# Linear attention with a gated feed-forward: tails of two batches computed together, loads held behind a transposition, and a reordered head

## The chip, the cores and the metric

The kernel runs on one core of one Trainium2 chip. The metric is the device time of one execution in microseconds (us), and a smaller number is better. Executions of this kernel agree within some 0.3%. The profile also records the clock that TensorE was granted, as a share of full speed.

## The reference, cut to what matters

Linear attention over 8 batches of 8 heads, with 576 rows of 64 columns each, feeds a layer with 2048 hidden units. Between the two matrix products of that layer stands a swish with one beta for each hidden unit. All inputs and the output are fp32.

```python
def phi(x):                              # elu(x) + 1
    return np.where(x > 0, x, np.exp(x) - 1.0) + 1.0
q_p, k_p = phi(q), phi(k)                # q, k, v: (8, 8, 576, 64)
kv  = np.einsum('bhsd,bhse->bhde', k_p, v)
z   = np.sum(k_p, axis=2)
num = np.einsum('bhsd,bhde->bhse', q_p, kv)
den = np.einsum('bhsd,bhd->bhs', q_p, z)[..., None] + 1e-06
x   = (num / den).transpose(0, 2, 1, 3).reshape(4608, 512)
h   = x @ w_in                           # (512, 2048)
g   = h * (1.0 / (1.0 + np.exp(-beta * h)))
out = g @ w_out                          # (2048, 512)
```

## The kernel before

A batch has 576 rows: four blocks of 128 and a tail of 64. The feed-forward runs in nine phases of 512 rows: one for the four blocks of each batch, and a last one for the eight tails together. While TensorE works on the feed-forward of batch b, the attention of batch b+1 is slipped in between its matmuls, by lists ("plans") that name a point in the stream and what to do there. The whole schedule is made by hand. The names that matter: `kv_bd` is kv with its denominators, `q_pT` the transposed phi(q), `xs` a normalised block of attention output and `xT` its transposition, `vaug` is v with a column of ones.

The numerators and their norm, with one matmul group for each block, the tail included:

```python
def num_mm(b, t):
    n = rows(t)                                   # 128, or 64 for the tail (t == 4)
    nps = att_banks()
    for p in range(KC):                           # KC = 4
        c0 = (p % 2) * 2 * (D + 1)
        nc.tensor.matmul(
            nps[:n, p // 2, c0 : c0 + 2 * (D + 1)],
            st[b, "qT"][:, t, p, :n],
            kv_bd[b % 2][p // 2][:, p % 2], ...)

def num_norm(b, t):
    n = rows(t)
    ...                                           # den + 1e-6, reciprocal, multiply -> xs
    if by_dma(b):                                 # batches 3 to 7
        nc.sync.dma_start_transpose(out=x_dst(b, t), in_=...xs...[:n])
```

The head loads batch 0 through GpSimd's queue, which in this kernel casts fp32 to bf16 on the way:

```python
    load_nine(k9, k)
    load_nine(q9, q, j1=4)
    ...
    load_nine(v9, v, j1=6)
    load_nine(v9, v, j0=6)
    load_nine(q9, q, j0=4)
    for i in range(4):
        nc.gpsimd.dma_start(out=w_in_sb[i], in_=w_in_v[:, :, i * 512 : (i + 1) * 512])
    load_w_out(0)
    ...
```

The plans of batches 1 and 2 (cut):

```python
    w_out_scale(2)
    phi(1, 1)                       # phi of k
    v_copy(1)
    phi(1, 0)                       # phi of q
    y_phase_wide(0, {
        4: [F(load_next, 3)],
        9: [F(kv_mm, 1), F(kv_evac, 1), F(w_out_scale, 3)],
        10: [F(q_trans, 1, 0, 1, wide=True), F(q_trans, 1, 2, 3, wide=True)],
        ...
    })
    h_phase(1, ..., {
        0: [F(x_trans, 1, 2), F(num_mm, 1, 4), F(num_norm, 1, 4)],
        1: [F(x_trans, 1, 3)],
        3: [F(x_trans, 1, 4)],
        ...
        12: [F(v_copy, 2), F(load_next, 4)],      # batch 4's k, q, v
    })
    ...
    y_phase_wide(1, {
        1: [F(phi, 2, 0), F(q_trans_dma, 2), F(phi, 2, 1)],
        6: [F(kv_mm, 2), F(kv_evac, 2)],
        11: [F(num_mm, 2, 0), F(num_norm, 2, 0)],
        12: [F(num_mm, 2, 1), F(num_norm, 2, 1), F(x_trans, 2, 0, wide=True)],
        ...
    })
```

Of the kernel before, what the change touches and what calls it, by code (L numbers as in the profile page):

```python
# [16 lines left out]
def kernel(  # L17
# [18 lines left out]
    NJ = 4  # L36
# [80 lines left out]
    def nine(a, spec):  # L117

        names = " ".join(spec)
        flat = a.rearrange("p a b c -> p (a b c)")  # L120
        size = {"h": HH, "j": N9, "d": D}
        n = size["h"] * size["j"] * size["d"]
        return flat[:, 0:n].rearrange(f"p ({names}) -> p {names}", **size)

    q9 = nine(xqk[0][:, 0], "hjd")
    k9 = nine(xqk[0][:, 1], "hjd")
    v9 = nine(vraw[0], "hjd")

    def load_nine(dst, src, h0=0, h1=HH, j0=0, j1=N9):
        for g in range(2):  # L130
            nc.gpsimd.dma_start(  # L131
                out=dst[g * TAIL : (g + 1) * TAIL, h0:h1, j0:j1, :].rearrange(
                    "p h j d -> p h (j d)"
                ),
                in_=src[0, g * HH + h0 : g * HH + h1, :, :]
                .rearrange("h (p j) d -> p h j d", j=N9)[:, :, j0:j1, :]
                .rearrange("p h j d -> p h (j d)"),
            )
# [4 lines left out]
    nc.vector.memset(g_sb[0][:, FC - 1, :], 0.0)  # L143
    clear_tail(1)
    nc.vector.memset(vraw[1][TAIL:P, :, NJ, :], 0.0)
    beta_row = consts.tile([FC, P], F32)
    nc.sync.dma_start(out=beta_row, in_=moe_beta.rearrange("(c p) -> c p", p=P))
# [3 lines left out]
    load_nine(k9, k)  # L151
    load_nine(q9, q, j1=4)
    make_identity(nc, identity)
    make_identity(nc, ident16)
    load_nine(v9, v, j1=6)
    load_nine(v9, v, j0=6)
    load_nine(q9, q, j0=4)
    for i in range(4):
# [9 lines left out]
    kv_bd = [  # L168
        [consts.tile([P, 2, 2, D + 1], BF16, name=f"kv_bd{i}{g}") for g in range(2)]
        for i in range(2)  # L170
    ]
    for i in range(2):
        for g in range(2):
            nc.vector.memset(kv_bd[i][g], 0.0)
# [32 lines left out]
    def w_out_scale(i, dve=True):  # L207
        for c in range(4):
            ff = 4 * i + c
            dst, src, by = w_out_sb[i][:, c, :], w_out_f[i][c // 2][:, c % 2, :], rbeta[:, ff : ff + 1]  # L210
            if dve:
# [36 lines left out]
    x0 = {0: q9, 1: k9}  # L248
# [4 lines left out]
    def exp0(a, j0, j1):  # L253
        if j0 == 0:
            st["e0", a] = work9("e", bufs=3)
        nc.scalar.activation(  # L256
            st["e0", a][:, j0:j1].rearrange("p j h d -> p h j d"), x0[a][:, :, j0:j1],
            ACTF.Exp,
        )

    def relu0(a, j0, j1):
        if j0 == 0:
            st["r0", a] = work9("r")
        nc.vector.tensor_scalar(
            st["r0", a][:, j0:j1].rearrange("p j h d -> p h j d"), x0[a][:, :, j0:j1],
# [3 lines left out]
    def phi0(a, j0, j1):  # L269
        nc.vector.tensor_tensor(  # L270
            st["p0"][a][:, j0:j1], st["r0", a][:, j0:j1], st["e0", a][:, j0:j1], ALU.min
        )

    def q_trans0(t, banks, c0):


        for jj in range(2 if t < NJ else 1):
            for a in range(2):
                for g in range(2):
# [4 lines left out]
                        st["p0"][0][gs, 2 * t + jj, 2 * a : 2 * a + 2, :],  # L284
# [4 lines left out]
    def q_out0(t, banks, c0, dve):  # L289
        n = rows(t)  # L290
        src = banks[:, :, c0 : c0 + 2 * P].rearrange("p g (a n) -> p g a n", a=2)
        dst = st[0, "qT"][:, t].rearrange("p (g a) n -> p g a n", g=2)
        copy(dst[:, :, :, :n], src[:, :, :, :n], dve)
# [5 lines left out]
    def kv_mm0(kvp, j0, j1, of_v):  # L299


        for j in range(j0, j1):
            for a in range(2):
                for g in range(2):
# [4 lines left out]
                        st["p0"][1][gs, j, 2 * a : 2 * a + 2, :],  # L309
# [6 lines left out]
    def kv_evac0(kvp):  # L316
        for g in range(2):
            for i in range(2):
                gs = slice(i * D, (i + 1) * D)
                copy(  # L320
                    kv_bd[0][g][gs, :, i, :],
# [29 lines left out]
    def kv_evac(b):  # L351
        for i in range(2):
            for g in range(2):
                gs = slice(g * D, (g + 1) * D)
                nc.vector.tensor_copy(  # L355
                    kv_bd[b % 2][i][gs, :, g, :], st[b, "kvp"][gs, 2 * i : 2 * i + 2, :]
                )
# [16 lines left out]
    def q_trans(b, *ts, wide=False, dve=False):  # L374

        n, m = rows(ts[0]), len(ts)
        tp = tr_bank(wide).rearrange("p (t c n) -> p t c n", t=2, c=KC)
# [7 lines left out]
        copy(st[b, "qT"][:, ts[0] : ts[0] + m, :, :n], tp[:, 0:m, :, :n], dve)  # L385
# [7 lines left out]
    def num_mm(b, t):  # L393
        n = rows(t)
        nps = att_banks()
        st[b, "n", t] = nps
        for p in range(KC):
            c0 = (p % 2) * 2 * (D + 1)
            nc.tensor.matmul(  # L399
                nps[:n, p // 2, c0 : c0 + 2 * (D + 1)],  # L400
                st[b, "qT"][:, t, p, :n],
                kv_bd[b % 2][p // 2][:, p % 2],
                start=True, stop=True, skip_group_check=True,
            )

    def num_norm(b, t):
        n = rows(t)
# [10 lines left out]
        if by_dma(b):  # L418
# [4 lines left out]
    def x_dst(b, t):  # L423
        if t < NJ:
            return xT[b % 3][:, t]
        return xT_tail[:, :, b * TAIL : (b + 1) * TAIL]

    def x_trans(b, t, wide=False, dve=False):
        n = rows(t)
# [51 lines left out]
    out0 = out[0:S, :].rearrange("(p j) m -> p j m", j=N9)  # L481

    def tail_rows(b):
        if b == 0:
            return out0[:, N9 - 1, :]
        return out[b * S + MAIN : (b + 1) * S, :]

    def store(b, t, y_sb):
        if b < B:
            if b == 0:  # L490
                for i in range(2):
                    nc.sync.dma_start(
                        out=out0[:, 2 * t + i, :], in_=y_sb[i * TAIL : (i + 1) * TAIL, :]
# [77 lines left out]


# [10 lines left out]
    def F(f, *a, **k):  # L583
        return lambda: f(*a, **k)

    begin(0)
    st["warm"] = mm_bank([P, 512])
    warm(10)
    beta_trans()
    make_beta()  # L590
    warm(20)
    st["p0"] = [
        nine(st[0, "p"][:, a].rearrange("p j (h d) -> p j h d", h=H), "jhd")
        for a in range(2)
    ]
    exp0(1, 0, 5)
    exp0(1, 5, N9)
    exp0(0, 0, 4)
    relu0(1, 0, 5)
    relu0(1, 5, N9)  # L600
    phi0(1, 0, 5)
    relu0(0, 0, 4)
    phi0(1, 5, N9)
    phi0(0, 0, 4)
    kvp = [mm_bank([P, 512]) for _ in range(2)]
    kv_mm0(kvp, 0, N9, False)
    qb = att_banks(BF16)
    q_trans0(0, qb, 0)
    q_trans0(1, qb, 256)
    q_out0(0, qb, 0, False)  # L610
    q_out0(1, qb, 256, False)
# [164 lines left out]
```

## Time and profile before

| | before |
|---|---|
| time, median of 3 runs | 296.43 us (296.33 to 296.48) |
| profiled execution | 296.85 us, of which 295.1 us is the span that the profile shows |
| TensorE busy | 283.9 us, 96% of the span |
| floor of the 1152 feed-forward units | 249 us |

The prediction below shows the lines that tell what bounds this kernel. Two more views follow. The first is the queue of the Sync engine (start in us, length in us, engine, operation) between 40 and 90 us, and the second is GpSimd over 52 to 66 us, where it issues batch 4's loads.

```profile
70.30 5.46 SPq L388 DMA_TRANSPOSE q_pT<-qk_p  x1
```

```profile
53.50 0.88 POOL L72 DMA_DIRECT2D xqk<-in_k_dram  x1 [1.58 <-ACT y_sb L513]
...
63.29 0.88 POOL L72 DMA_DIRECT2D vraw<-in_v_dram  x1 [2.28 <-DMA xqk<-in_q_dram]
```

The transposition of batch 2's q is issued at 70.30 us and is on the queue for 5.46 us. By the view of its tile it has landed 9.0 us after its issue, at 79.3, which is exactly when TensorE's first numerators of batch 2 start. Batch 4's loads are issued from 53.50 us on and are still moving then.

### The profile page before, as it was taken

Reading aid. Unit: us, or ns where it says so; the run is one execution under the profiler, and the core shown is the slowest. Engines: PE = TensorE matmul, PEld = TensorE weight load, DVE = VectorE, ACT = ScalarE, POOL = GpSimd, SP = SyncE. Lnnn points to the kernel's source line nnn. Section 1 sums busy time; section 2 is a strip of 40 time slices with the busy share of each in tenths; the row PEclk is TensorE's granted clock in tenths of the full one; section 3 lists DMA queues with packets and bytes.
Section 4 is the critical chain, followed back from the end, with each engine's and each line's share of the span. In section 5 each row is a group of like instructions: output and inputs, shape, how many; then the busy total and the mean of one; then the engine's idle time right before and its main releaser. Section 6 shows DMA issues by size and latency. Waiting matters only on the chain.

```text
span 295.1 us, 4750 instructions
## 1 busy us (share of the span) xinstructions
PE 283.9 (96%) x1891; PEld 143.9 (49%) x1912; DVE 124.0 (42%) x261; ACT 175.1 (59%) x234; POOL 52.7 (18%) x72
## 2 busy tenths in 40 slices
PE   8879999999999999999999999999999999999994
PEld 3557445644465544445444544454445444444444
DVE  4765488504365174616461646154715400110012
ACT  2788786889988780778087907790770077018500
POOL 8924474540003200330023000000000000000000
PEclk9999999999999999999999999999999999999999
DMA  7999999999637993699369945024502400120032
GB/s 103 196 207 343 256 272 192 256 193 192 89 142 100 175 131 113 130 174 154 98 129 159 159 109 124 2 71 116 127 0 72 118 36 0 38 90 16 0 73 71
DMA packets 72310, 37.09 MB, mean 126 GB/s; under 512 B 40912, under 2 KB 66784, under 8 KB 72288
## 3 DMA queue, kind: packets, MB, share of 16 engines
q0 software_dynamic: 38912, 20.45, 47.9%
q1 hardware_dynamic: 33216, 16.20, 22.9%
q8 instruction: 15, 0.25, 0.3%
q10 hardware_dynamic: 160, 0.13, 0.2%
q14 instruction: 7, 0.06, 0.1%
HBM read 36.71 MB, written 9.44 MB: 156 GB/s over the span
## 4 chain that ended last, share of the span: by engine, by line
PE 76%; DMA 9%; POOL 4%; ACT 4%; issue 4%; DVE 1%; ACTq 0%; POOLq 0%; DVEq 0%
PE mm L453 37%; PE mm L505 33%; DMA xT<-in_moe_w_out_dram 5%; DMA vraw<-in_v_dram 4%; PE att L399 3%; ACT e L229 2%; POOL xqk L131 1%; PE att L344 1%; PE mm L537 1%; POOL w_in L159 1%; ACT L229 1%; POOL vraw L131 1%; ACT g L445 1%; DVE qk_p L242 0%; POOL xqk L111 0%
## 5 line engine op out<-in xcount | busy, mean ns | idle before, releaser
L445 ACT ACTIVATE g<-mm,beta_c 128x512 bf16<-128x512 f32 (+2 forms) x156 | 97.3, 633 | 88.4 <-PE mm L453 88.1
L505 PE MATMUL mm<-w_out,g 128*128 128x512 bf16 x541 | 126.7, 379 | 1.2 <-issue 0.3
L453 PE MATMUL mm<-xT,w_in 128*128 128x512 bf16 (+2 forms) x560 | 108.1, 349 | 1.4 <-DMA w_in<-in_moe_w_in_dram 1.1
L453 PEld LDWEIGHTS <-w_in 128*128 128x128 bf16 x656 | 61.9, 98 | 62.4 <-DMA w_in<-in_moe_w_in_dram 1.2
L505 PEld LDWEIGHTS <-g 128*128 128x128 bf16 x560 | 53.0, 98 | 58.2
L515 DVE COPY y_sb<-mm 128x512 f32<-128x512 f32 x27 | 18.7, 691 | 70.6 <-PE mm L505 69.1
L229 ACT ACTIVATE e<-xqk 128x2560 bf16<-128x2560 bf16 x14 | 31.9, 2329 | 0.1
L415 DVE TENSOR_TENSOR xs<-att,rden 128x512 bf16<-128x512 f32 (+1 forms) x40 | 27.6, 689 | 1.4
L242 DVE TENSOR_TENSOR qk_p<-r,e 128x2560 bf16<-128x2560 bf16 x14 | 20.9, 1490 | 13.1 <-ACT e L229 12.4
L355 DVE CAST kv_bd<-att 64x130 bf16<-64x130 f32 x28 | 8.2, 292 | 32.2 <-PE att L344 31.8
L72 POOL DMA_DIRECT2D vraw<-in_v_dram x7 | 6.4, 909 | 84.2 <-DVE vaug L370 78.5
L413 DVE TENSOR_SCALAR den<-att 128x8 f32<-128x8 f32 (+1 forms) x40 | 6.5, 161 | 32.0 <-PE att L399 31.9
L399 PE MATMUL att<-kv_bd,q_pT 128*128 128x130 bf16 (+1 forms) x160 | 15.8, 221 | 1.1 <-DVE kv_bd L370 0.7
L399 PEld LDWEIGHTS <-q_pT 128*128 128x128 bf16 (+1 forms) x160 | 11.6, 100 | 10.7 <-DVE xs L415 2.4
L453 PE MATMUL mm<-xT_tail,w_in 128*128 128x512 bf16 x63 | 13.9, 379 | 0.1
L237 DVE TENSOR_SCALAR r<-xqk 128x2560 bf16<-128x2560 bf16 x14 | 11.6, 834 | 3.8 <-DMA xqk<-in_q_dram 2.3
L575 PE MATMUL mm<-g 128*128 128x512 bf16 x34 | 9.9, 452 | 1.2 <-DVE g L143 1.2
L229 ACT ACT_TABLE_LOAD x7 | 9.0, 1283 | 0.1
L414 DVE RECIPROCAL rden<-den 128x8 f32<-128x8 f32 (+1 forms) x40 | 8.1, 202 | 1.4
L72 POOL DMA_DIRECT2D xqk<-in_k_dram x7 | 6.9, 984 | 6.3 <-DMA w_in<-in_moe_w_in_dram 2.8
L76 POOL DMA_DIRECT2D xqk<-in_k_dram x7 | 7.4, 1057 | 1.5 <-DMA w_in<-in_moe_w_in_dram 1.3
L256 ACT ACTIVATE e<-xqk 128x1280 bf16<-128x1280 bf16 (+1 forms) x4 | 4.4, 1155 | 5.4 <-DMA xqk<-in_k_dram 5.3
(71 smaller groups left out, 140.0 us busy)
## 6 DMA issues: line engine op xcount, KB each, us to landing
out_dram<-y_sb SPq DMA_DIRECT2D x28, 256.0 KB, 2.3
xqk<-in_k_dram POOLq DMA_DIRECT2D x7, 512.0 KB, 10.7
xqk<-in_q_dram POOLq DMA_DIRECT2D x7, 512.0 KB, 11.3
vraw<-in_v_dram POOLq DMA_DIRECT2D x7, 512.0 KB, 11.3
w_in<-in_moe_w_in_dram POOLq DMA_DIRECT2D x4, 512.0 KB, 11.0
g<-in_moe_w_out_dram POOLq DMA_DIRECT2D x4, 512.0 KB, 10.9
out_dram<-y_sb SPq DMA_DIRECT2D x14, 128.0 KB, 5.2
xqk<-in_moe_w_out_dram POOLq DMA_DIRECT2D x2, 512.0 KB, 14.4
```

What stands on the lines that cost most here:

```text
L72: eng.dma_start(out=dst[:, :, 0:NJ, :].rearrange("p h j d -> p h (j d)"), in_=src[b, :, 0:MAIN, :].rearrange("h (p j) d -> p h (j d)", j=NJ),)
L229: nc.scalar.activation(st[b, "e", a][:, h0:h1], xqk[b % NX][:, a, h0:h1], ACTF.Exp)
L237: nc.vector.tensor_scalar(st[b, "r", a][:, h0:h1], xqk[b % NX][:, a, h0:h1], 0.0, 1.0, ALU.max, ALU.add)
L242: nc.vector.tensor_tensor(st[b, "p"][:, a].rearrange("p j (h d) -> p h j d", h=H)[:, h0:h1], st[b, "r", a][:, h0:h1], st[b, "e", a][:, h0: ...
L355: nc.vector.tensor_copy(kv_bd[b % 2][i][gs, :, g, :], st[b, "kvp"][gs, 2 * i : 2 * i + 2, :])
L399: nc.tensor.matmul(nps[:n, p // 2, c0 : c0 + 2 * (D + 1)], st[b, "qT"][:, t, p, :n], kv_bd[b % 2][p // 2][:, p % 2], start=True, stop=True ...
L415: nc.vector.tensor_mul(xs[:n], nv[:, :, :, 0:D], rden[:n, :, :, None].to_broadcast([n, 2, 4, D]))
L445: nc.scalar.activation(g_sb[b % 2][:, ff, c0:c1], hp[:, c0:c1], ACTF.Silu, scale=beta_c[:, ff : ff + 1],)
L453: nc.tensor.matmul(hp[:, c0:c1], w_in_sb[ff // 4][:, kc, (ff % 4) * P : (ff % 4 + 1) * P], x[:, t0:t1, kc, :] if b < B else x[:, kc, c0:c1 ...
L505: nc.tensor.matmul(yp, g_sb[b % 2][:, ff, t * P : (t + 1) * P], w_out_sb[ff // 4][:, ff % 4, :], start=(ff == 0), stop=(ff == FC - 1),)
L515: nc.vector.tensor_copy(y_sb, yp)
L575: nc.tensor.matmul(st["warm"], g_sb[0][:, FC - 1, 0:P], g_sb[0][:, FC - 1, :], start=True, stop=True, skip_group_check=True,)
```

## The change

The intent was to take the last few us out of an already full TensorE. The tails of two neighbouring batches are computed as one block of 2 x 64 rows (joint tails), so half of the tail work vanishes. Batch 4's loads are held until batch 2's q has been transposed, by a one-element copy on GpSimd that reads the transposed q. In the head, k arrives through two queues, and kv and q are taken in smaller pieces. In batch 1, q is transposed ahead of kv. In batch 2, copies of x^T move from ScalarE to VectorE. (Beta's small load moves from Sync's queue to ScalarE's.) The diff, cut to its core:

```diff
 # the head
+    load_nine(k_last, k, KF, N9, eng=nc.sync)          # 4 of 9 parts of k, fp32, Sync's queue
-    load_nine(k9, k)
-    load_nine(q9, q, j1=4)
+    load_nine(x9[1][:, :, 0:KF], k, 0, KF)             # KF = 5
+    load_nine(x9[0][:, :, 0:QF], q, 0, QF)             # QF = 4
...
-    warm(20)
+    warm(15)
...
 # kv copied out in two pieces (was four)
 def kv_evac(b):
-    for i in range(2):
-        for g in range(2): ...
+    for g in range(2):
+        gs = slice(g * D, (g + 1) * D)
+        nc.vector.tensor_copy(kv_bd[b % 2][gs, :, g, :], st[b, "kvp"][gs])
...
 # joint tails
 def num_mm(b, t):
     for p in range(KC):
         c0 = (p % 2) * 2 * (D + 1)
+        for i in range(1 if t < NJ else 2):
+            bb, n, r0 = (b, P, 0) if t < NJ else (b - 1 + i, TAIL, i * TAIL)
             nc.tensor.matmul(
-                nps[:n, p // 2, c0 : c0 + 2 * (D + 1)],
-                st[b, "qT"][:, t, p, :n],
-                kv_bd[b % 2][p // 2][:, p % 2],
+                nps[r0 : r0 + n, p // 2, c0 : c0 + 2 * (D + 1)],
+                st[bb, "qT"][:, t, p, :n],
+                kv_bd[bb % 2][:, p],
...
-        if by_dma(b):
+        if by_dma(b) or t == NJ:
...
 # held loads
+    def hold(a):
+        nc.gpsimd.tensor_copy(held, a)
+    def held_load(b, n):
+        hold(st[n, "qT"][0:1, NJ, KC - 1, 0:1])
+        load_next(b)
...
 # batch 1
-    v_copy(1)
     phi(1, 0)
+    v_copy(1, 0, HH)
+    v_copy(1, HH, H, dve=False)
-        9: [F(kv_mm, 1), F(kv_evac, 1), F(w_out_scale, 3)],
-        10: [F(q_trans, 1, 0, 1, wide=True), F(q_trans, 1, 2, 3, wide=True)],
+        10: [F(q_trans, 1, 0, 1, 2, 3), F(kv_mm, 1), F(kv_evac, 1), F(w_out_scale, 3, 2)],
...
 # batch 2
-            12: [F(v_copy, 2), F(load_next, 4)],
+            12: [F(v_copy, 2)],
-        6: [F(kv_mm, 2), F(kv_evac, 2)],
+        6: [F(kv_mm, 2), F(kv_evac, 2), F(held_load, 4, 2)],
-        12: [..., F(x_trans, 2, 0, wide=True)],
+        12: [..., F(x_trans, 2, 0, wide=True, dve=True)],
```

## The prediction

> **What bounds the kernel now.** I read the page first, then TensorE's waits, TensorE's groups with shapes kept apart, the chain that ended last, and the time-ordered view of the stretches where the chain leaves TensorE. The page:
>
> ```profile
> PE 283.9 (96%) x1891; PEld 143.9 (49%) x1912; DVE 124.0 (42%) x261; ACT 175.1 (59%) x234; POOL 52.7 (18%) x72
> PE   8879999999999999999999999999999999999994
> DMA  7999999999637993699369945024502400120032
> ```
>
> TensorE is busy for 283.9 of 295.1 us, and only the first two or three slices and the last have room. Busy is not peak, so I checked the rate: in the chain of the last feed-forward phase 37 matmuls of 512 columns take 7.99 us, 0.216 us each. There are 1152 such units (9 phases x 64 for each of the two projections), so 1152 x 0.216 = 249 us cannot be touched; nor does the diff touch them. In the steady state the chain reaches the kv products at 97.91, 127.77, 157.63 us: 29.86 us for each batch, of which 27.65 us are the 128 projections. A change can win only (a) attention matmuls on TensorE, (b) the head, (c) the few waits in the first three batches. The page's DMA row says that the 16 DMA engines are full from about 4 us on, so (b) is also a question of bytes. The groups, then the stretches of TensorE in order of time (start, length, what, idle before it):
>
> ```profile
> L399 PE MATMUL att<-kv_bd,q_pT 128*128 128x130 bf16 x128 | 12.4, 220 | 1.1 <-DVE kv_bd L370 0.7 <-DMA q_pT<-qk_p 0.3
> L399 PE MATMUL att<-kv_bd,q_pT 128*64 128x130 bf16 x32 | 3.3, 226 | 0.0
> L433 PE MATMUL mm<-identity,xs 64*128 64x64 bf16 x12 | 0.9, 192 | 0.0
> ```
> ```profile
> 7.49 3.16 ACT L256 ACTIVATE e<-xqk 128x1280 bf16<-128x1280 bf16 x3 [5.25 <-DMA xqk<-in_k_dram]
> ```
> ```profile
> 17.16 1.07 PE L453 MATMUL mm<-xT,w_in 128*128 128x128 bf16 x16 [1.10 <-DMA w_in<-in_moe_w_in_dram]
> ...
> 43.23 0.82 PE L344 MATMUL att<-vaug,qk_p 128*64 128x65 bf16 x40 [0.28 <-DVE vaug L370]
> ...
> 45.75 0.62 PE L380 MATMUL att<-identity,qk_p 128*128 128x128 bf16 x8 [0.28 <-DVE kv_bd L355]
> ...
> 53.29 0.42 PE L399 MATMUL att<-kv_bd,q_pT 128*64 128x130 bf16 x4
> 53.64 0.61 PE L453 MATMUL mm<-xT,w_in 128*128 128x256 bf16 x4
> ```
> ```profile
> 79.33 0.41 PE L399 MATMUL att<-kv_bd,q_pT 128*128 128x130 bf16 x4 [0.34 <-DMA q_pT<-qk_p]
> ...
> 83.07 0.38 PE L433 MATMUL att<-identity,xs 128*128 128x128 bf16 x4 [0.61 <-ACT xT L372]
> ```
>
> A tail of 64 rows takes TensorE's stream 53.64 - 53.29 = 0.35 us for its four numerators. A full block of 128 rows takes 0.23 us in the same view (47.07 to 47.30): half the rows cost more. The tail's four transposes take another 0.22 us (55.28 to 55.50), for batches 0, 1 and 2; later ones are transposed by DMA. The other rows give every wait worth naming: the head waits for k (ScalarE idle 5.25 us), then for the first quarter of w_in (1.10); batch 1 waits 0.28 for v and 0.28 for kv copied out; batch 2 waits 0.34 for its q, transposed by DMA, and 0.61 for a ScalarE copy.
>
> **What the Trainium skill says.** *TensorEngine Tiling (Array Packing)*, Key Properties: different tiles can execute weight loads and matmuls in parallel, and switching the tiling mode drains the engine. The trace agrees: the 40 kv products on alternating column halves take 0.75 us, 0.019 each, below what 65 columns cost one at a time (65/512 x 0.216 = 0.027), while the lone tail, which has nothing on the other half, costs 0.35. *DMA: Bandwidth & Descriptors*, Latency and other measured facts, puts the first byte at about 600 ns for DMAs issued by Sync or Scalar and about 1 us for GpSimd's. Here beta, issued by Sync at 0.75 us, lands in 1.5 us, and GpSimd's first k load, issued at 1.25, has moved only some 12 KB by 3.0 us. The same page, Terms and the queue model: all these DMAs run on the same 16 engines, which take the queues in turn. So a second queue starts k earlier but adds no bandwidth once the engines are full, and they are.
>
> **The change, part by part.**
>
> *1. Joint tails.* Numerators of an even batch's tail are postponed and computed with the odd one's, in the two column halves of one bank. The order of instructions shows the two halves alternating. Even tails vanish: 4 x 0.35 = 1.4 us of stream. An odd batch's 8 matmuls now overlap in pairs: estimated from the kv rate as 4 x (130/512 x 0.216 = 0.055, plus some 0.03 of weights not hidden, which is what the lone tail shows: 0.35/4 - 0.055) = 0.35, as before. So 0 there, and 1.4 in all. Tail transposes of batches 0, 1, 2 go to DMA: 3 x 0.22 = 0.66. The DMA ones have until the last feed-forward phase, at 264 us. VectorE normalises 4 tails fewer, 4 x 1.05 us, beside other work. Sum on the path: **2.0 us**.
>
> *2. The head.* The last four ninths of k come uncast through Sync's queue from about 0.75 us, before GpSimd can start. The bytes read are the same, so I take only the earlier start: Sync's first bytes at about 2.05 us against 2.75, 0.7 us. The chain from k to the first numerators also gets shorter: kv's last pieces follow only one transposition of q, and q's second copy and the fifth of the exps go behind. From 7.49 to 13.55 this chain is 6.06 us; in the new order I get about 12.4 for the numerators and 14.9 for x^T. But the projections wait for w_in, 17.12 us by its last of 16 landing counts. The DMA queue is full ahead of it, so it comes only with the bytes: estimated 0.7 to 1.0 us earlier, chosen **0.8**. Nearly all of the shortened chain is then spent waiting for w_in.
>
> *3. Batch 0's first projection.* x^T of block 1 is now ready while w_in lands, so the 0.31 us wait at 19.28 us should mostly go: **0.2**. (The tail's 0.57 is in part 1.)
>
> *4. Batch 1.* q's 16 transposes move ahead of kv, phi ahead of the copy of v, and v's copy is split between VectorE and ScalarE. The two waits of 0.28 and a gap of some 0.16 are 0.7 us of possible gain. But the four norms follow kv_bd and two w_out pieces on VectorE: followed through, the first numerators come some 0.7 us sooner, and the first x transposes only 0.35, as they wait for the norm. Copying kv out in two pieces of 64x260 takes an estimated 0.8 to 0.9 us against 1.2. I count **0.35**.
>
> *5. Batch 2.* Batch 4's loads are held until q of batch 2 has been transposed. That transpose is issued at 70.30 and takes 5.46 us on the queue against 2.93 later, undisturbed. The 0.34 us wait goes: **0.34**. x^T copies move from ScalarE, which is behind with exps until 81.85, to VectorE. The 0.61 us becomes a wait for VectorE's own norms, of an estimated 0.3: **0.3**.
>
> Sum: 2.0 + 0.8 + 0.2 + 0.35 + 0.64 = 4.0 us, all of it in series, as each lies on TensorE's stream or its waits. 296.43 - 4.0 = **292.4 us**, 1.3% faster.
>
> **Rivals.** *A. The DMA takes the head's gain.* If the fp32 k takes more of the engines (it is written at twice the bytes), w_in lands as before and part 2 is 0: 293.2. For it: the 16 engines are at 9 of 10 from 4 us on. Against: the uncast w_out loads run at some 390 GB/s written and the cast ones at some 190, twice that read, so reading seems to set the rate. *B. Two queues overlap better than one*, and w_in lands up to 1.4 us earlier (262 KB of bf16 leave its queue, at 190 GB/s): 291.8. *C. Joint tails do not overlap:* 8 lone matmuls at 0.0875 are 0.70 us, 0.35 more for each of four pairs, so part 1 shrinks by 1.4: 293.8. Against it stands the kv rate. If, the other way, pairs run at nearly 0.06, another 0.4 is won. *D. VectorE becomes the bound at batches 1 and 2*, as it takes on copies of x^T between norms: parts 4 and 5 fall by some 0.8. *E. The held loads come late:* batch 4's 1.7 MB need some 9 us after about 75 us and are first used at 103: hidden.
>
> **Range and chances.** A and C together give 294.6; B with the better joint tails 291.4, and with all waits gone about 290.8. I take **290.8 to 294.6**. Faster by over 2% needs under 290.5, more than every part at its best: 0.06. Slower by over 2% would need a new stall of 10 us, and I see no loop that could give one: 0.02. Within 2%: 0.92.
>
> **What would show it.** Part 1: the row of 128*64 matmuls stays at 32, with none for even batches, a joint tail between 0.25 and 0.40 us, no 64x64 transposes of xs, and periods alternating between 29.86 and some 29.5. Part 2: ScalarE's first exp at about 6.4 us in place of 7.49, the first projection at about 16.4, and still a wait for w_in of 1 us or more in front of it. Part 4: first numerators of batch 1 some 0.7 us sooner than the shift alone, with TensorE then waiting for VectorE. Part 5: no wait for q_pT, a shorter wait at batch 2's second x transposes. The prediction is wrong if the joint tail takes 0.7, if w_in lands where it did, or if a new wait of over 1 us stands in batches 1 or 2, whose hand-made order I followed only by adding durations.

## The result

The changed kernel took 293.32 us in the median of four runs (293.12 to 293.62). The kernel before took 296.46 us in four runs of the same rounds. The ratio is 0.9894, with a 95% interval of 0.9877 to 0.9912: 1.1% faster, which is within 2%. A ratio here is the mean time of one kernel's fast runs over that of the other's fast runs of the same rounds, so it is not quite the ratio of the medians quoted beside it.

The profiled execution took 293.12 us with a span of 291.3 us, 3.8 us shorter than the span before. That difference flatters the change a little, because the profiled execution of before was 0.4 us above its own median.

The page of the changed kernel: span, busy time of each engine, and the DMA engines in 40 slices of 7.28 us.

```profile
span 291.3 us, 4693 instructions
PE 281.8 (97%) x1875; PEld 142.6 (49%) x1895; DVE 119.2 (41%) x239; ACT 173.5 (60%) x228; POOL 50.7 (17%) x73
...
DMA  8999999994899986798379955032503400120033
```

TensorE gave up 2.1 us of busy time and 1.7 us of idle time, and remained the bound at 97%. The DMA row has a hole in its 10th slice, from 65.5 us on: 4, then 8 and 9, where the row of before has 9, then 6 and 3. Batch 4's loads have moved from before batch 2's transposition to after it.

The longest of TensorE's waits in the changed kernel, but for the one at its very start (waited for, us in total, times, longest):

```profile
PE att L395 <- DVE qk_p L242: 0.7, 1, 0.7
PE mm L475 <- DVE xT L385: 0.5, 1, 0.5
PE mm L455 <- DVE xs L437: 0.4, 1, 0.4
```

In this trace no wait for w_in, for q_pT by DMA or for v is left, but the first line, 0.7 us for VectorE's phi of batch 1's q, is new. Next the row of tail numerators (operation, shape, count, then busy us and mean ns of one), and TensorE in order of time where the first joint tail stands:

```profile
L421 PE MATMUL att<-kv_bd,q_pT 128*64 128x130 bf16 x32 | 1.7, 227 | 0.0
```

```profile
42.89 1.07 PE L395 MATMUL att<-identity,qk_p 128*128 128x128 bf16 x16 [0.70 <-DVE qk_p L242]
...
45.98 0.40 PE L421 MATMUL att<-kv_bd,q_pT 128*128 128x130 bf16 x4 [0.30 <-ACT q_pT L387]
...
52.37 0.42 PE L421 MATMUL att<-kv_bd,q_pT 128*64 128x130 bf16 x8
52.72 0.61 PE L475 MATMUL mm<-xT,w_in 128*128 128x256 bf16 x4
```

The count of 128*64 matmuls is still 32, but their busy time is 1.7 us where the same row of before has 3.3. The eight matmuls of the joint tail take 52.72 - 52.37 = 0.35 us of the stream, as long as the four of one tail did.

The lines that answer to the waits of the head and of batch 2, again on TensorE in order of time, then the Sync engine's queue and GpSimd:

```profile
15.67 0.61 PE L475 MATMUL mm<-xT,w_in 128*128 128x128 bf16 x8 [0.52 <-DVE xT L385]
```

```profile
77.70 0.40 PE L421 MATMUL att<-kv_bd,q_pT 128*128 128x130 bf16 x4
...
81.53 0.39 PE L455 MATMUL att<-identity,xs 128*128 128x128 bf16 x4
```

```profile
69.16 3.08 SPq L407 DMA_TRANSPOSE q_pT<-qk_p  x1
```

```profile
74.06 0.18 POOL L598 COPY held<-q_pT 1x1 bf16<-1x1 bf16 x1 [22.16 <-DMA q_pT<-qk_p]
74.30 0.88 POOL L72 DMA_DIRECT2D xqk<-in_k_dram  x1
```

In front of the first projection the wait for w_in has become one for VectorE's x^T, half as long. Batch 2's q is transposed in 3.08 us on the queue, lands 4.9 us after its issue, and is there 3.6 us before it is needed. Only then do the held loads go out. The second block's transpositions at 81.53 us no longer wait for ScalarE.

Comparing the two traces point by point shows where the time came from (all in us from the start of the span). A second trace of the same kernel, in the experiments, shows that the points of the head vary from run to run by more than a microsecond:

| point on TensorE, or as told | before | after | gained so far |
|---|---|---|---|
| ScalarE's first exp of k | 7.49 | 7.31 | 0.18 |
| first numerators of batch 0 | 13.55 | 13.14 | 0.41 |
| first projection of batch 0 | 17.16 | 15.67 | 1.49 |
| first numerators of batch 1 | 47.07 | 45.98 | 1.09 |
| first projection of batch 1 | 52.53 | 51.61 | 0.92 |
| second projection of batch 1 begins | 67.61 | 66.48 | 1.13 |
| first numerators of batch 2 | 79.33 | 77.70 | 1.63 |
| first projection of batch 2 | 85.25 | 83.17 | 2.08 |
| kv of batch 3 | 97.84 | 94.97 | 2.87 |
| kv of batch 7 | 217.28 | 213.57 | 3.71 |

The head's early lead of 1.49 us shrinks to 0.92 by batch 1. Batch 2 adds 0.95 between 67 and 85 us. From batch 3 on every second period is some 0.4 us shorter: the kv products of the changed kernel start at 94.97, 124.85, 154.27, 184.15 and 213.57 us, so periods of 29.88 and 29.42 alternate, where all of before's are 29.86.

### The profile page after: what moved, and what is told of

It is laid out like the page before. It is cut to its first block, busy times and chain, and to the rows that moved or that the text cites. A ratio compares the mean times of both kernels' runs of the same rounds, so it can differ in the third digit from the quotient of the medians.

```text
span 291.3 us, 4693 instructions
## 1 busy us (share of the span) xinstructions
PE 281.8 (97%) x1875; PEld 142.6 (49%) x1895; DVE 119.2 (41%) x239; ACT 173.5 (60%) x228; POOL 50.7 (17%) x73
## 4 chain that ended last, share of the span: by engine, by line
PE 82%; DMA 9%; POOL 4%; DVE 2%; issue 1%; ACT 1%; POOLq 0%; DVEq 0%
PE mm L527 37%; PE mm L475 37%; DMA xqk<-in_moe_w_out_dram 5%; DMA g<-in_moe_w_out_dram 4%; PE att L421 3%; PE att L362 2%; POOL xqk L135 1%; PE mm L559 1%; PE att L475 1%; POOL w_in L162 1%; DVE qk_p L242 1%; POOL vraw L135 1%; ACT q_pT L387 1%; DVE xs L437 0%; PE att L395 0%
## 5 line engine op out<-in xcount | busy, mean ns | idle before, releaser
L437 DVE TENSOR_TENSOR xs<-att,rden 128x512 bf16<-128x512 f32 x36 | 24.9, 692 | 1.2
L372 DVE CAST kv_bd<-att 64x260 bf16<-64x260 f32 x14 | 6.0, 427 | 33.0 <-PE att L362 32.9
L435 DVE TENSOR_SCALAR den<-att 128x8 f32<-128x8 f32 x36 | 5.9, 163 | 29.5 <-PE att L421 29.2
L421 PEld LDWEIGHTS <-q_pT 128*128 128x128 bf16 (+1 forms) x160 | 10.7, 100 | 9.7 <-DVE xs L437 1.9
L421 PE MATMUL att<-kv_bd,q_pT 128*128 128x130 bf16 (+1 forms) x160 | 14.3, 222 | 0.8 <-DVE kv_bd L385 0.4
L608 PE MATMUL mm<-g 128*128 128x512 bf16 x29 | 9.3, 477 | 1.3 <-DVE g L145 1.2
L436 DVE RECIPROCAL rden<-den 128x8 f32<-128x8 f32 x36 | 7.3, 203 | 1.2
L72 POOL DMA_DIRECT2D xqk<-in_k_dram x7 | 6.9, 984 | 3.0 <-DMA w_in<-in_moe_w_in_dram 1.5
L475 PE MATMUL att<-xT,w_in 128*128 128x512 bf16 x32 | 7.2, 379 | 0.0
L72 POOL DMA_DIRECT2D xqk<-in_q_dram x7 | 6.3, 904 | 3.9 <-ACT w_out L214 2.0
```

Of the source, the lines that this page charges most:

```text
L72: eng.dma_start(out=dst[:, :, 0:NJ, :].rearrange("p h j d -> p h (j d)"), in_=src[b, :, 0:MAIN, :].rearrange("h (p j) d -> p h (j d)", j=NJ),)
L421: nc.tensor.matmul(nps[r0 : r0 + n, p // 2, c0 : c0 + 2 * (D + 1)], st[bb, "qT"][:, t, p, :n], kv_bd[bb % 2][:, p], start=True, stop=True, ...
L436: nc.vector.reciprocal(rden[:n], den[:n])
L437: nc.vector.tensor_mul(xs[:n], nv[:, :, :, 0:D], rden[:n, :, :, None].to_broadcast([n, 2, 4, D]))
L475: nc.tensor.matmul(hp[:, c0:c1], w_in_sb[ff // 4][:, kc, (ff % 4) * P : (ff % 4 + 1) * P], x[:, t0:t1, kc, :] if b < B else x[:, kc, c0:c1 ...
L608: nc.tensor.matmul(st["warm"], g_sb[0][:, FC - 1, 0:P], g_sb[0][:, FC - 1, :], start=True, stop=True, skip_group_check=True,)
```

## The experiments

Twelve kernels ran, in four groups. Each group shared a chip and its runs of the kernel before, so kernels are compared by their ratio to before, and directly only within a group. All results were correct.

**Group 1, the tails.** The theory was that joint tails are worth 2.0 us by themselves, and that the head's early start is lost at batch 1, which waits for w_out and v. The rivals were that tails and loads interact, and that the joint tail needs its two halves to alternate.

*The changed kernel again*, unedited, as a control.

> The changed kernel itself, timed again as the yardstick for the others on this chip. Both theories: 293.3 us, 3.1 us under the kernel before, give or take 0.3. Its trace also tells whether the landing of w_in at 15.5 us (17.1 before) and the wait of 0.7 us for batch 1's phi of q are the same from run to run.

It took 293.01 us (292.80 to 293.10, clock 1.0 in all four runs), a ratio of 0.988 (0.9866 to 0.9894). Its profile shows something the first one did not, in the order of time on TensorE, first in the head and then at batch 1:

```profile
16.96 0.62 PE L475 MATMUL mm<-xT,w_in 128*128 128x128 bf16 x8 [1.79 <-DMA w_in<-in_moe_w_in_dram]
```

```profile
51.43 0.60 PE L475 MATMUL mm<-xT,w_in 128*128 128x256 bf16 x4
```

Here TensorE waited 1.79 us for w_in and started the first projection at 16.96 us, 1.3 us later than in the first profile and nearly as late as before. Yet batch 1's projections started at 51.43, sooner than 51.61, and the whole took 292.94 us. The 0.7 us wait for VectorE's phi is absent here. So when the first projection starts does not decide when batch 1 starts, within these 1.3 us.

A third trace with the same program up to here, that of the loads not held (below), shows what batch 1 follows instead. VectorE's scaling of the last half of w_out's third part, which waits for that half to land, in the control and then in that trace:

```profile
38.73 0.88 DVE L212 TENSOR_SCALAR w_out<-g,rbeta 128x512 bf16<-128x512 f32 x2 [0.21 <-DMA g<-in_moe_w_out_dram]
```

```profile
39.83 1.28 DVE L212 TENSOR_SCALAR w_out<-g,rbeta 128x512 bf16<-128x512 f32 x2 [0.29 <-DMA g<-in_moe_w_out_dram]
```

The landing is 1.10 us later there, and batch 1's projections are 1.26 us later (52.69 us against 51.43), although the first projection is only 0.58 us later (17.54 against 16.96).

*Joint tails alone, in the kernel before.*

```diff
 # the kernel before
-            nc.tensor.matmul(nps[:n, ...], st[b, "qT"][:, t, p, :n], kv_bd[b % 2][p // 2][:, p % 2], ...)
+            for i in range(1 if t < NJ else 2):
+                bb, n, r0 = (b, P, 0) if t < NJ else (b - 1 + i, TAIL, i * TAIL)
+                nc.tensor.matmul(nps[r0 : r0 + n, ...], st[bb, "qT"][:, t, p, :n], kv_bd[bb % 2]..., ...)
...
-        if by_dma(b):
+        if by_dma(b) or t == NJ:
...
 # and no numerators, norms and transpositions of even tails in the plans
```

> The kernel before with the joint tails alone. Theory (each part of the sum stands by itself, tails are pure TensorE stream): 4 x 0.35 us of numerators of even batches and 3 x 0.22 us of transposes go, 2.0 us, so 294.4 us. Rival (what is won in batches 0 and 1 is lost again, because batch 1 waits for transfers that end at the same time whatever TensorE does): batch 0's 0.57 us are lost, 1.4 us stay, so 295.0 us.

It became slower, which neither expectation had: 298.82 us, 1.0063 (1.0036 to 1.0091). The order of time on TensorE, then the Sync engine's queue:

```profile
82.09 0.41 PE L400 MATMUL att<-kv_bd,q_pT 128*128 128x130 bf16 x4 [3.93 <-DMA q_pT<-qk_p]
```

```profile
54.31 1.32 SPq L420 DMA_TRANSPOSE xT_tail<-xs  x1
69.46 6.93 SPq L388 DMA_TRANSPOSE q_pT<-qk_p  x1
```

The 0.34 us wait for batch 2's q has become 3.93 us. That transposition is issued 0.84 us sooner than in the kernel before, but it lands later: it is on the queue for 6.93 us in place of 5.46, and the view of its tile has it landed after 12.6 us in place of 9.0. Batch 4's v is issued at 65.15 us here, and at 63.29 before. A new DMA transposition, that of the joint tail, is issued at 54.31 us among batch 4's loads and lands only after 8.1 us (as late as in the changed kernel, where those loads are held). Batch 4's k takes 16.5 us from its issue to its landing, against 15.1 before. That it is this transposition which delays those loads, and they the next transposition, is the likely chain but is argued from the order of events; what is shown is that holding the loads removes the wait (below).

There is a second cost. From 83.12 us on, 1.0 us after the idle stretch, the granted clock is at half for 3.41 us. The three runs with a mean clock of 0.994 lie at 298.76 to 299.12 us, one with 0.989 at 299.87, and the two with 1.0 at 296.91 and 297.05. So the wait seems to cost twice: in itself, and by some 1.9 us for the clock that follows it. A stretch of 3.41 us at half clock in which TensorE is the bound should cost half of it, 1.7 us, which fits; but only a run with the lowered clock was profiled, so how long the two runs with 1.0 waited is not known.

*The changed kernel with separate tails.*

```diff
-            for i in range(1 if t < NJ else 2):
-                bb, n, r0 = (b, P, 0) if t < NJ else (b - 1 + i, TAIL, i * TAIL)
+            for i in range(1):
+                bb, n, r0 = b, rows(t), 0
...
-        if by_dma(b) or t == NJ:
+        if by_dma(b):
...
 # and the even tails back in their places in the plans
```

> The changed kernel with each batch's tail by itself, as before. Theory (tails are stream): 2.0 us are given back, 295.3 us, only 1.1 us under the kernel before. Rival (batch 0's share is lost in batch 1's wait anyway): 1.4 us given back, 294.7 us, and the first projection of batch 1 starts at most 0.1 us later than in the changed kernel, though batch 0's runs 0.57 us longer.

It took 295.45 us, 0.9973 (0.995 to 0.9996). Three of its six runs had a clock of 0.992 to 0.994; the other three lie at 294.83 to 295.07, against 292.80 to 293.10 for the control. Run for run at a clock of 0.998 or more, the joint tails are worth 2.0 us in the changed kernel, which is the prediction's figure for them.

*The halves one after the other*: all four matmuls of the first tail, then all four of the second.

```diff
-        for p in range(KC):
-            c0 = (p % 2) * 2 * (D + 1)
-            for i in range(1 if t < NJ else 2):
+        for i in range(1 if t < NJ else 2):
+            for p in range(KC):
+                c0 = (p % 2) * 2 * (D + 1)
```

> The changed kernel with the joint tail's eight matmuls in another order: four for the first column half, then four for the second. Theory (the halves overlap only when they alternate): the joint tail takes 0.70 us in place of 0.35, 4 x 0.35 = 1.4 us slower, 294.7 us. Rival (it is the postponing, not the alternation, that matters, or the engine overlaps them in any order): 0.35 us and 293.3 us as before.

It took 293.13 us, 0.9888 (0.9875 to 0.99), the same as the control.

```profile
52.31 0.43 PE L419 MATMUL att<-kv_bd,q_pT 128*64 128x130 bf16 x8
52.68 0.61 PE L473 MATMUL mm<-xT,w_in 128*128 128x256 bf16 x4
```

The joint tail takes 52.68 - 52.31 = 0.37 us. The halves overlap in this order as well, so the alternation that the prediction leant on is not needed. The single matmuls of a lone tail, in the trace of the kernel before, start 0.056 to 0.081 us apart, 0.061 in the median, so four take some 0.24 us (an estimate), and the remaining 0.11 of its 0.35 us belong to the edges of the group: the next matmul starts 0.154 us after the fourth.

**Group 2, the hold, the head, batch 1.**

*Joint tails and held loads, in the kernel before*: the edit of the tails alone, and this one on top.

```diff
+    def held_load(b, n):
+        hold(st[n, "qT"][0:1, NJ, KC - 1, 0:1])      # hold() as in the changed kernel
+        load_next(b)
...
-            12: [F(v_copy, 2), F(load_next, 4)],
+            12: [F(v_copy, 2)],
...
-        6: [F(kv_mm, 2), F(kv_evac, 2)],
+        6: [F(kv_mm, 2), F(kv_evac, 2), F(held_load, 4, 2)],
```

> The kernel before with the joint tails and the held loads of batch 4, nothing else. The tails alone gave 298.8 us, 2.3 us slower than before, with TensorE waiting 3.9 us for batch 2's q transposed by DMA at a lowered clock after it. Theory (the tails win 2 us of stream, but TensorE then meets the transpose of q earlier while batch 4's loads are on the same engines; the hold takes that away): the wait for q_pT is gone and the time is 294.2 us or less. Rival (the tail's own DMA transpose at 54 us delays q's, whatever the loads do): the wait stays at 3 us or more, 298 us.

It took 294.86 us, 0.9949 (0.9937 to 0.9961), 0.7 us more than the theory allowed. The wait for q_pT is gone, and the transposition is on its queue for 3.06 us. What TensorE waits for instead:

```profile
PE att L344 <- DVE vaug L370: 1.2, 1, 1.2
...
PE att L434 <- ACT xT L372: 1.1, 1, 1.1
```

The first, for v, belongs to batch 1. The second shows what the copies of x^T on VectorE are for: with ScalarE making them, batch 2 waits 1.1 us at its second block; in the changed kernel that wait is absent. (The changed kernel differs in more than that; see part 5 below.)

*The changed kernel with batch 4's loads not held.*

```diff
-            12: [F(v_copy, 2)],
+            12: [F(v_copy, 2), F(load_next, 4)],
-        6: [F(kv_mm, 2), F(kv_evac, 2), F(held_load, 4, 2)],
+        6: [F(kv_mm, 2), F(kv_evac, 2)],
```

> The changed kernel with batch 4's loads issued where they were before. The prediction on record: 0.34 us given back, 293.4 us. Theory now: the wait for q_pT comes back at 3 to 4 us, plus up to 1 us for the clock that falls in it: 296 to 298 us, no better than the kernel before. The hold is then worth more than any other part.

It took 298.48 us, 1.0074 (1.006 to 1.0089), a little over what was expected. Against the changed kernel's 0.988 to 0.9894 this makes the hold worth 1.8 to 1.9%, or 5.3 to 5.8 us. The order of time on TensorE, and the stretch of 78 to 86 us (length, busy us of PE, PEld, DVE, ACT and POOL with counts, granted clock, DMA share, GB/s; the DMA share adds up the times of the packets and can pass 1):

```profile
82.61 0.62 PE L421 MATMUL att<-kv_bd,q_pT 128*128 128x130 bf16 x4 [3.66 <-DMA q_pT<-qk_p]
```

```profile
78.00:86.00 8.00, 4.34 (x24) 2.28 (x23) 1.59 (x6) 4.57 (x5) 0.00 (x0) 0.79 0.39 43
```

The same picture as with the tails alone: a wait of 3.66 us for q, and half the clock for 3.41 us from 82.04 us on, 0.57 us before the wait ends, which is why the mean clock of these 8 us is 0.79. In those 8 us TensorE issues 24 matmuls where the changed kernel issues 67.

This trace also settles a rival: that the wait appears because TensorE comes to the transposition earlier. Here the transposition is issued at 70.23 us, no earlier than in the kernel before (70.30), and yet it lands after 12.3 us in place of 9.0. What is later in both kernels with joint tails and loads not held is batch 4's v, issued at 65.35 us here and at 65.15 with the tails alone, against 63.29 before.

*k whole through GpSimd's queue*, cast, in the changed kernel.

```diff
-    load_nine(k_last, k, KF, N9, eng=nc.sync)
-    load_nine(x9[1][:, :, 0:KF], k, 0, KF)
+    load_nine(x9[1], k, 0, N9)
...
```

> The changed kernel with k whole through GpSimd's queue, as before. The prediction on record: 0.8 us given back, 293.8 us. Theory now (batch 1 waits for w_out and v, which land when they land; a later head is absorbed there): the first projection starts up to 1 us later, batch 1's first projection within 0.2 us of the changed kernel's 51.4 to 51.6, and the time is 293.0 to 293.3 us.

It took 293.72 us, 0.991 (0.9897 to 0.9923), with a clock of 0.992 to 0.994 in all five runs. The first projection starts at 16.73 us and batch 1's at 51.94, 0.3 to 0.5 us later than in the two traces of the changed kernel, which is more than the theory allowed. ScalarE's first lines, of this kernel and of the changed one:

```profile
6.70 3.33 ACT L263 ACTIVATE e<-xqk 128x1280 bf16<-128x1280 bf16 x4 [4.45 <-DMA xqk<-in_k_dram]
```

```profile
7.31 1.27 ACT L266 ACTIVATE e<-xqk 128x1280 bf16<-128x1280 bf16 x1 [5.07 <-DMA xqk<-in_k_dram]
```

With one queue k is there at 6.70 us, sooner than the 7.31 with two. One pair of traces is not enough here, as this point varies from run to run, but the other traces bear it out. The five with k whole on GpSimd's queue (this one, the kernel before and the three runs made from it without the new head) have the first exp at 6.70 to 7.49 us, and the kernel before is the latest of them. The nine with k on two queues have it at 7.31 to 8.30. So nothing shows that the second queue brought it forward. The loads from issue to landing (KB each, then us), GpSimd's in the changed kernel and in this one:

```profile
xqk<-in_k_dram POOLq DMA_DIRECT2D x2, 160.0 KB, 4.6
```

```profile
xqk<-in_k_dram POOLq DMA_DIRECT2D x2, 288.0 KB, 4.3
```

GpSimd's part of k takes as long as the whole of it did. What else was moved can be worked out from the stretch of 0 to 8 us, first this kernel and then the changed one:

```profile
0.00:4.00 4.00, 2.77 (x7) 1.04 (x8) 2.48 (x11) 1.49 (x2) 2.96 (x9) 1.00 0.34 48
4.00:8.00 4.00, 4.00 (x17) 1.60 (x16) 0.87 (x3) 1.30 (x2) 3.85 (x10) 1.00 1.27 187
```

```profile
0.00:4.00 4.00, 2.77 (x7) 1.04 (x8) 2.48 (x11) 1.49 (x2) 2.96 (x9) 1.00 0.47 101
4.00:8.00 4.00, 4.00 (x14) 1.45 (x13) 0.68 (x2) 0.69 (x1) 3.85 (x10) 1.00 1.30 202
```

By 8 us the changed kernel has moved 4 us x (101 + 202) GB/s = 1212 KB and this one 4 x (48 + 187) = 940 KB, 272 KB less (an estimate, as k lands within that stretch in both). Four ninths of k are 131,072 numbers, which fill 524 KB as fp32 and 262 KB as bf16, so the difference is about the 262 KB by which the fp32 copy is larger. That fits an earlier start used up by the doubled size; no run varies the size alone. An earlier k did not bring the first numerators forward either: they start at 13.47 us here and at 13.14 in the changed kernel, as TensorE waits 1.3 us for v in this head and its clock falls at 11.91 us. The ratio, 0.2 to 0.3% worse than the changed kernel's, is not a clean measure of the split, as the clock dropped in every run of this kernel (12 to 16 us: mean 0.58).

*Batch 1's order undone* in the changed kernel: kv ahead of q's transposition, v copied by VectorE alone between the two phi.

```diff
     phi(1, 1)
+    v_copy(1)
     phi(1, 0)
-    v_copy(1, 0, HH)
-    v_copy(1, HH, H, dve=False)
...
-        10: [F(q_trans, 1, 0, 1, 2, 3), F(kv_mm, 1), F(kv_evac, 1), F(w_out_scale, 3, 2)],
+        9: [F(kv_mm, 1), F(kv_evac, 1), F(w_out_scale, 3)],
+        10: [F(q_trans, 1, 0, 1), F(q_trans, 1, 2, 3)],
```

> The changed kernel with batch 1's q, kv and v in the order of before. The prediction on record: 0.35 us given back, 293.4 us. Theory now (before and after, batch 1 hangs on v landing at about 41.8 us; in the old order v's copy stands ahead of the last phi and kv ahead of the transposes): batch 1's first numerators come at 46.5 to 47 us as in the kernel before, against 45.8 to 46.0, so 1.0 us given back, 294.0 us.

It took 293.23 us, 0.9891 (0.9878 to 0.9904): nothing is lost. TensorE in batch 1:

```profile
45.60 0.40 PE L421 MATMUL att<-kv_bd,q_pT 128*128 128x130 bf16 x4
...
51.28 0.60 PE L475 MATMUL mm<-xT,w_in 128*128 128x256 bf16 x4
```

The first numerators come at 45.60 us and the projections at 51.28, no later than with the new order (45.98 and 51.61; 51.43 in the control). The reordering is worth nothing that these runs can resolve.

**Group 3, the hold alone, and two refinements of batch 1.**

*Held loads alone, in the kernel before* (the edit of the tails and hold experiment without the tails).

> The kernel before with the held loads of batch 4 alone. The prediction on record: the 0.34 us wait for q_pT goes, 296.1 us. Theory now (the hold is worth most where TensorE comes early: 4 us with the joint tails, 5 us in the changed kernel, but in the kernel before the transpose was late by 0.34 us only): the same, 296.1 us, and part of the 0.34 us may return as wait for the x copies on ScalarE. Rival (the hold has a worth of its own of 4 to 5 us): 292 us.

It took 296.17 us, 0.9991 (0.9979 to 1.0003). The wait for q is gone, and TensorE's list has 1.1 us for ScalarE's copy of x^T in its place (0.6 before). With this run the four combinations on the kernel before are complete:

| ratio to the kernel before | loads not held | loads held |
|---|---|---|
| separate tails | 1 | 0.9991 |
| joint tails | 1.0063 | 0.9949 |

Alone the tails cost 1.9 us and the hold gains 0.3, which is not clear of noise (its interval reaches 1.0003); together they gain 1.5.

*phi of batch 1's k ahead of w_out's third part*, in the changed kernel, as its new wait of 0.7 us is for VectorE, which scales w_out first:

```diff
-    w_out_scale(2)
     phi(1, 1)
+    w_out_scale(2)
     phi(1, 0)
```

> The changed kernel with phi of batch 1's k ahead of the scaling of w_out's third part on VectorE, which stands waiting for that part to land at 37.3 and 38.6 us. Theory (VectorE's queue behind the landing holds up batch 1's q): the wait of 0.6 to 0.7 us in front of q's transposes goes, its first numerators come 0.4 to 0.6 us earlier, 292.7 us. Rival (v, landing at 41.8 us, holds up kv anyway): no gain, 293.2 us.

The profiled run took 292.52 us: the wait is gone, and the projections of batch 1 start at 51.02 us, 0.6 sooner than in the first trace of the changed kernel and 0.4 sooner than in the control's. But the median is 293.58 us, 0.9919 (0.9894 to 0.9945), as four of six runs had a clock of 0.994 and spread from 293.04 to 295.48. A gain as small as the one in the trace cannot be seen under that spread.

*In addition the first copy of batch 1's transposed q on VectorE.*

```diff
                 st[b, "qT"][:, ts[i] : ts[i] + m, :, :n], tp[:, i : i + m, :, :n],
-                False
+                len(ts) > 1 and i == 0,
```

> The same with the first of the two large copies of batch 1's transposed q on VectorE, which stands idle for 1.5 us there, in place of ScalarE. Theory (the first numerators wait 0.30 us for ScalarE's second copy, and the last scalings of w_out come late behind it): both waits go, another 0.5 us, 292.2 us. Rival (kv copied out on VectorE comes later by the 0.9 us of the copy): no gain over the run before it, 292.7 us.

It took 292.90 us, 0.9882 (0.9867 to 0.9896), no different from the control's 0.988.

**Group 4, a combination.** Several of the changed kernel's relatives show a half clock for 3.41 us in the head as well. The stretch of 12 to 16 us in the trace of the last experiment, then in that of this one, which adds five warming matmuls (20, as in the kernel before) and divides v's copy as 5 and 3 heads:

```diff
-    warm(15)
+    warm(20)
-    v_copy(1, 0, HH)
-    v_copy(1, HH, H, dve=False)
+    v_copy(1, 0, 5)
+    v_copy(1, 5, H, dve=False)
```

> The last run's kernel (phi of batch 1's k first, one copy of q on VectorE) with 20 warming matmuls instead of 15, as before the change, and v's copy split 5 to 3 heads instead of 4 to 4. Theory (with 15, TensorE idles 0.6 to 1.4 us before k's phi and in about half of the runs the granted clock falls to half for 3.4 us at 11 to 15 us, a mean of 0.994): no run under 0.997, a narrower spread, 292.4 us, 0.9 under the changed kernel. Rival (the clock falls because of the light work at 10 to 15 us, not the warming): runs at 0.994 as before and 292.9 us.

```profile
12.00:16.00 4.00, 3.80 (x38) 2.47 (x37) 2.47 (x8) 3.21 (x6) 2.61 (x4) 0.59 1.26 207
```

```profile
12.00:16.00 4.00, 2.84 (x32) 1.66 (x31) 3.20 (x13) 3.84 (x7) 2.41 (x5) 1.00 1.25 207
```

It took 292.94 us (292.51 to 293.21), 0.9876 (0.986 to 0.9893). No run had a clock under 0.998. Its point estimate is the best of all, but the interval covers the changed kernel's, so it is not shown to beat it.

All runs, each against the kernel before of its own group:

| kernel | median us | ratio | 95% |
|---|---|---|---|
| changed kernel | 293.32 | 0.9894 | 0.9877 to 0.9912 |
| changed kernel again | 293.01 | 0.988 | 0.9866 to 0.9894 |
| tails alone | 298.82 | 1.0063 | 1.0036 to 1.0091 |
| separate tails | 295.45 | 0.9973 | 0.995 to 0.9996 |
| halves in turn | 293.13 | 0.9888 | 0.9875 to 0.99 |
| tails and hold | 294.86 | 0.9949 | 0.9937 to 0.9961 |
| loads not held | 298.48 | 1.0074 | 1.006 to 1.0089 |
| k by one queue | 293.72 | 0.991 | 0.9897 to 0.9923 |
| batch 1's order undone | 293.23 | 0.9891 | 0.9878 to 0.9904 |
| hold alone | 296.17 | 0.9991 | 0.9979 to 1.0003 |
| phi of k first | 293.58 | 0.9919 | 0.9894 to 0.9945 |
| and q's copy on VectorE | 292.90 | 0.9882 | 0.9867 to 0.9896 |
| and longer warming | 292.94 | 0.9876 | 0.986 to 0.9893 |

## Why the prediction was right or wrong, point by point

**The total** was right: 292.4 us was predicted with a range of 290.8 to 294.6, and 293.32 us was measured. The sum of 4.0 us compares with 3.8 in the profiles and 3.1 in the medians. Three of its terms were mis-sized and partly made up for each other, so that the total came so close is in part luck.

**Part 1, joint tails, 2.0 us**: right in size. The separate tails cost 2.0 us when put back, the joint tail takes 0.35 us as estimated, and the periods alternate between 29.88 and 29.42 where 29.86 and 29.5 were named. Two things in it were wrong. The split of the 0.35 us into 4 x (0.055 + 0.03 of weights not hidden) is not what the runs show: starts are 0.061 us apart in the median, and some 0.11 us sits at the edges. And "The DMA ones have until the last feed-forward phase" looked only at when the result is needed. It left out that a new transposition goes into a queue in which another one, needed at once, comes next among full DMA engines. With the tails alone TensorE waited 3.93 us for that next one, and the kernel became slower; that the new transposition is the cause is the likely chain, not a shown one.

**Part 2, the head, 0.8 us**: the step "I take only the earlier start: Sync's first bytes at about 2.05 us against 2.75, 0.7 us" failed. The first exp came at 7.31 us and not at 6.4, and in none of the nine traces with two queues sooner than that, while with one queue it came at 6.70 to 7.49. Sync's bytes did start sooner, but GpSimd's part of k, with 160 KB in place of 288, took 4.6 us to land as before. That the fp32 copy's doubled bytes took back what the earlier start gave fits the bytes moved. Rival A, that the fp32 k takes more of the engines, had the mechanism, though not its consequence for w_in, which TensorE could use 1.5 us sooner in one profile and 0.2 sooner in the control's. One reading behind this part was off as well: by 3.0 us GpSimd's queue had moved some 29 KB in the kernel before, not 12.

When TensorE could start on w_in did not matter for what followed, which is the second failure: the text took it that every part lies "in series". Batch 1 ran into data of its own. In the changed kernel the chain of waits goes through w_out's third part:

```profile
27.55 11.04 DMA g<-in_moe_w_out_dram
...
39.27 0.77 DVE w_out L212
40.04 2.80 DVE qk_p L242 x2
```

The DMA of this part's last piece ends at 38.6 us, VectorE scales it and then makes phi, and only then, at 42.89 us, can TensorE transpose q. The scaling begins at 37.32 us in the changed kernel and at 37.34 in the one before, so this end did not move, and a head that is 1.5 us early waits for it. Where this landing came 1.10 us later, in the trace of the loads not held, batch 1 came 1.26 us later.

**Part 3, 0.2 us**: the wait of 0.31 us for ScalarE's copy of block 1's x^T is gone, but TensorE now waits 0.44 us for VectorE's norm of the same block, ahead of its transposition. Nothing was gained in that trace.

**Part 4, batch 1, 0.35 us**: about nothing, by the run that undid the order. Rival D, that VectorE sets the pace there, was true in part: the new 0.7 us wait is for VectorE, and taking phi ahead of w_out removed it, for 0.4 to 0.6 us in that trace. In the control, whose head is 1.3 us later, the wait is absent without it.

**Part 5, batch 2, 0.64 us**: 0.95 in the profiles (0.34 and 0.61, both waits entirely gone), and 5.3 to 5.8 us by the run that left the loads unheld. The prediction sized the hold by the wait that the kernel before showed, 0.34 us. It should have been sized by the wait that the other parts would have made of it. No run separates the copies of x^T on VectorE; that they remove the 1.1 us wait seen with tails and hold is an inference.

**The sum by place**, the prediction's own terms put where they fall, against the table of points:

| stretch | predicted | measured |
|---|---|---|
| up to batch 1's projections: one even tail 0.57, head 0.8, part 3 0.2, batch 1 0.35 | 1.92 | 0.92 |
| to batch 1's second projection: tail transposition | 0.22 | 0.21 |
| to batch 2's projections: part 5 | 0.64 | 0.95 |
| to the end: tails of batches 2, 4, 6, 0.57 + 2 x 0.35 | 1.27 | 1.72 |

So 1.0 us is missing in the head and batch 1, outside the tails if these are worth their 2.0 us there too, and 0.75 us of that came back in batch 2 and in the later pairs, which gain 0.44 us each (29.86 - 29.42) where 0.35 was named.

**The rivals.** C fell: the halves overlap, in either order. E held: the loads issued from 74.3 us on are never waited for. A, B and D are told above; where TensorE could start on w_in differs by 1.3 us between two runs of the same kernel, as much as A and B differ, so the runs don't decide between those two.

**The signs of being wrong.** The joint tail did not take 0.7 us, and no new wait of over 1 us stands in batches 1 or 2. But in the control w_in let TensorE start at 16.96 us, nearly "where it did" (17.16), and the whole was as fast. So that sign said nothing about the total, for the reason given in part 2.

**"Slower by over 2% would need a new stall of 10 us, and I see no loop that could give one"** stood. But a stall of 3.7 us, with half the clock for 3.41 us, was one missing edit away, in the run with the loads not held.

**Left open** are the chain by which the tail's transposition delays batch 4's loads, whether the last three variants gain anything, and what decides whether the clock drops in the head. TensorE is busy 2.25 to 2.83 us of the 4 us from 8 to 12 us in the four traces with a drop, but 2.54 in one without.

## What to carry to other kernels

Before a transfer is moved or added, look at what stands behind it in its queue and when that is needed: here joint tails, which put a small DMA whose own result has 200 us of time ahead of another that is needed at once, turned a 0.34 us wait into 3.9 us. Size a part of a change by the wait that the other parts would cause without it, not by the wait seen before, and test parts in pairs: here one part alone lost 1.9 us, the other alone gained 0.3, and together they gained 1.5. A lead in the head is worth only what the next landing lets through, so look for the first later point whose data does not move.

## What the Trainium skill lacked or had wrong

- *TensorE: Matmul & The Clock Gate*, Why this matters for your kernels, warns of TensorE gaps of over some 3 us, after which the clock falls to half. The traces agree: with gaps of 3.66 and 3.93 us it was at half for 3.41 us, once from 0.57 us before the end of the gap, once from 1.0 us after it. A rule of single gaps does not cover all of it: in four traces the clock fell between 11 and 16 us where no single gap was over 1.5 us. (The page does tell elsewhere, of another kernel, that frequent short idle times can do this, so it is only this section that lacks it.)
- *DMA: Bandwidth & Descriptors*, DMA Transpose (X-bar), has no figure for how a small transposition stretches beside other loads. The transposition of batch 2's q was on its queue for 3.06 to 3.08 us with the loads held, and for 5.46 to 6.93 us among them, and landed after 4.9 us in the one case and after 9.0 to 12.6 us in the other.
- The same page, Latency and other measured facts, gives the earlier first byte of Sync's queue. It does not say that this can be lost when the data then has to come uncast: k was ready at 7.31 to 8.30 us by two queues (nine traces) and at 6.70 to 7.49 us by one (five).
- *TensorEngine Tiling (Array Packing)*, Key Properties, says that a change of tiling mode drains the engine, without a cost. A group of 8 half-width matmuls here takes 0.35 us, of which some 0.11 (an estimate from starts 0.061 us apart) is at its edges; that the drain is what fills them is not shown. That different tiles run in parallel is borne out, with the halves alternating (0.35 us) or one after the other (0.37).
